# Attention and two FFN layers on one core: 128 operations get new ranks in a hand-run planner, with new planner durations, one early weight conversion instead of three, and a dummy activation

## The chip, the cores and the metric

The kernel runs on one core of a Trainium2 chip. The metric is the device time of one execution in microseconds (us), given as the median of the runs. One further execution was taken with the hardware profiler on; all rows below come from it.

## The reference

```python
scores = scale * q @ k.T                       # 4 batches, 8 heads, 576 x 576, head size 64
thresh = max(scores, -1) - tau                 # keep only scores near the row's maximum
attn = softmax(where(scores >= thresh, scores, -1e9))
x = (attn @ v) -> (2304, 512)                  # tokens x model
h = x @ w_in                                   # 512 x 2048
x = (h * sigmoid(1.702 * h)) @ w_out           # layer 1
h = x @ w_in2
out = (h * tanh(softplus(h))) @ w_out2         # layer 2
```

## The kernel before

Everything is float32; the FFN products are made from two fp32r parts each (a rounded part and the rest).

**Attention** runs over 72 groups: for each of 16 (batch, head pair) entries four full tiles of 128 queries of both heads, and for every second entry one mixed tile. A group has a score product on PE (L591), then for each of two heads on DVE a scaled copy with row minimum (L614), on POOL a threshold (L618), on ACT the exponential (L621), on DVE the masking with row sum (L624). Two groups later PE transposes the result (L660, L665), ACT copies it out of PSUM (L680), and PE multiplies it with v (L703, L728). Only one set of score banks exists, so the next group's L591 waits for both L614 of this one.

**The FFN layers** run over 48 pairs of 128-wide slices of the hidden layer, 24 for each layer, in 3 token blocks of 768 with 8 pairs each. A pair has seven products on PE (L829), copies and sums (L851, L843), the activation (L846), a split into two parts (L878, L881, L884), and the output product (L904 and L907, or L949).

**Weights** come as 64-bit words and are converted once by `conv_w` (L358): two ACT steps (L377, L379), two short DVE steps (L383, L386), one POOL step (L389), one DVE step (L391). `stage` (L408) converts the two halves of a pair and stores them to DRAM. `weights` (L418) either converts a pair of layer 1 in the ring `sv` (4 buffers, 2 to a pair) or loads it from DRAM (L427), and then splits it into the tiles `win` and `wout` (L444, L445, L449, L466, L467). `EARLY` says how many pairs are converted ahead: pair 0 through `weights`, pairs 1 and 2 through `stage` in the ring `sg`, each then loaded back into `sv`. `load_xs` (L499) loads, normalises and splits the tokens of a block.

**The order** of the work is made by the class `Order`. Each step is given to `add` with its engine, a duration, what it reads and writes, and a rank. `run` (L95) lets the steps run on a clock of its own: an engine that is free takes, of the steps that are ready, the one with the lowest rank; PE pays `TURN` for a change between score, transpose and product work; steps marked `port` on DVE and POOL exclude each other. `LAT` holds the delay from a step to a reader on another engine. The order that results is the order of issue on each engine; on the chip the engines wait for each other by semaphores, so the plan's times themselves don't reach the chip, only its order. Attention ranks are 0 to about 74, `load_xs(0)` has 80, FFN ranks start at 10000.

The lines on which the steps hang are L165, L421 and, for the dummy activation, the reads of "qsc" in L627:

```python
ready[a] = max(ready[a], end + lat + SLACK)
...
if n == 0 or len(EARLY) <= n < KP:
    vals = stage(1, k, rank, deps, svs)
...
    [kns, kn, kn + (1,), "qsc"], [kp, ksum + (col,)], rank, port=True)
```

Of the kernel before, what the change touches and what calls it, by code (L numbers as in the profile page):

```python
# [14 lines left out]
AF = mybir.ActivationFunctionType  # L15
# [17 lines left out]
FI = 20  # L33
HALF = 384
NHS = 4
SLACK = 0.0
AHEAD = 2
NSS = 6
EARLY = (1, 2, 3)
XR = 80  # L40
S0 = 8
S1 = 2
SR = 0.0
WR = 0.0


class Order:
# [7 lines left out]

    LAT = {
        "PE": {"PE": 0.0, "ACT": 0.27, "DVE": 0.2, "POOL": 0.27, "SP": 0.2},
        "DVE": {"PE": 0.26, "ACT": 0.13, "DVE": 0.13, "POOL": 0.16, "SP": 0.2},
        "ACT": {"PE": 0.22, "ACT": 0.08, "DVE": 0.15, "POOL": 0.16, "SP": 0.2},
        "POOL": {"PE": 0.22, "ACT": 0.08, "DVE": 0.15, "POOL": 0.1, "SP": 0.2},  # L60
        "SP": {"PE": 0.95, "ACT": 0.95, "DVE": 0.95, "POOL": 0.95, "SP": 0.95},
# [2 lines left out]
    def __init__(self):  # L64
        self.ops = []
        self.writer = {}
        self.readers = {}
        self.fill = None
        self.port = set()
        self.mode = {}  # L70

    def add(self, eng, dur, fn, r=(), w=(), rank=0.0, deps=(), nbytes=None, port=False, steps=1, mode=0):
        n = len(self.ops)
        if mode:
            self.mode[n] = mode
        if port:
            self.port.add(n)
        before = set(deps)
        for key in r:
            if key in self.writer:  # L80
                before.add(self.writer[key])
        for key in w:
            if key in self.writer:
                before.add(self.writer[key])
            before.update(self.readers.get(key, ()))
        for key in r:
            self.readers.setdefault(key, []).append(n)
        for key in w:
            self.writer[key] = n
            self.readers[key] = []  # L90
        before.discard(n)
        self.ops.append((eng, dur, fn, before, rank, nbytes, steps))
        return n

    def run(self):  # L95
# [20 lines left out]
        while done < n_ops:  # L116
# [45 lines left out]
            order.append((t, i))  # L162
            for a in after[i]:
                lat = self.LAT[e][self.ops[a][0]] if dur or nbytes else 0.0
                ready[a] = max(ready[a], end + lat + SLACK)  # L165
                left[a] -= 1
                if not left[a]:
                    heapq.heappush(future[self.ops[a][0]], (ready[a], a))
# [42 lines left out]
def attention_then_two_ffn_kernel(  # L211
# [86 lines left out]
    def t_mm(n, k=1):  # L298
        return k * (max(n, 256) * 0.4167e-3 + 0.0125)
# [4 lines left out]
    def t_act(n, ptr=0, psum=True):  # L304
        return (0.05 if psum else 0.09) + n * 0.833e-3 + 0.093 * ptr
# [262 lines left out]
    def qk(tl, rank):  # L568
# [6 lines left out]
        def mm():  # L575
# [18 lines left out]
                yield  # L594

        add("PE", 1.02, mm, [h[2] for h in kqt], [("sc", i) for i in range(4)], rank,
            steps=4 if full else 10, mode=1)
        return [(sc[i][:, :, 0:SH], [("sc", 2 * i), ("sc", 2 * i + 1)]) for i in range(2)]

    def softmax_a(sums, ksum, col, rank, bank, pair, i):  # L600
# [196 lines left out]
        reopen("g", i, [("p", i)] + ([("pmt", i)] if i < 2 else []))  # L797
    for i in range(3):
        reopen("x2", i, [("vr", i)])
    open_hb = add("SP", 0.0, open_h, deps=scored, rank=-10.0)  # L800
    load_xs(0, XR)
    for n, at in enumerate(EARLY):
# [12 lines left out]
    def hidden(n, rank):  # L815
# [16 lines left out]
                    yield  # L832

        def product(p, dst, kd, start):
            i = add("PE", t_mm(HALF, 6) + 0.03, lambda: mm(p, dst, start),
                    [("xq", p), ("win", n % 3, p)], [kd], rank + PO[p] / 8, [open_hb] if n == 0 else [], steps=6)
            firsts.setdefault(n, i)

        def h(i, j, x, kx, y=None, ky=None):
            ht, kh = hs[i]  # L840
            cs = slice(j * HALF, (j + 1) * HALF)
            if y is not None:
                add("DVE", t_dve(HALF), lambda: nc.vector.tensor_tensor(ht[:, cs], x(), y, ALU.add),  # L843
                    [kx, ky], [kh + (j,)], rank - 4.0)
            add("ACT", t_act(HALF),
                lambda: nc.scalar.activation(ht[:, cs], x() if y is None else ht[:, cs], fn),  # L846
                [kx] if y is None else [], [kh + (j,)], rank - 4.0)

# [86 lines left out]
    def out2(n, rank):  # L935
# [6 lines left out]
        for q, (i, ts) in enumerate(order):  # L942
            g, kg = units[i]

            def mm(i=i, ts=ts, g=g):
# [7 lines left out]
                        )  # L953
                        yield

            add("PE", 3 * len(ts) * t_mm(512), mm, kg + [("wout", n % 3)], [ka2[t] for t in ts],
                rank + (q + 0.5) / len(order), steps=3 * len(ts))
        if k == KP - 1:
            for t in range(6):
# [82 lines left out]
```

## Time and profile before

| | us |
|---|---|
| median of 3 runs | 1038.72 |
| lowest and highest | 1037.98, 1039.24 |
| profiled execution, its own time | 1037.93 |
| its span, first to last instruction | 1036.2 |
| PE busy | 1020.9 (99%) |
| DVE busy | 832.7 (80%) |
| ACT busy | 659.7 (64%) |
| POOL busy | 168.7 (16%) |

The time of the profiled execution is 1.7 us over its span. The granted clock is full throughout. PE's matmuls are pipelined, and the ends of their records are modelled, so a busy PE may still lose time between two matmuls; the waits of its weight loads (PEld) show such places. Times in rows are us from the span's start.

### The profile page before, as it was taken

How to read it: one execution, taken by the hardware profiler on the slowest of the kernel's cores; microseconds unless marked ns; L12 is line 12 of the kernel's file. 1: busy time of each engine (PE TensorE's matmuls, PEld its weight loads, DVE VectorE, ACT ScalarE, POOL GpSimd, SP SyncE). 2: the span in 40 equal slices, each digit the busy share in tenths (PEclk: the TensorE clock that was granted, in tenths of full speed). 3: DMA queues.
4: the chain of work that ended last, by engine and by line, in shares of the span. 5: the costliest groups of instructions: out<-in, count | busy, mean ns of one | idle time of the engine just before them, and what ended most of it. 6: DMA issues, size and time to landing. Idle time of an engine off the chain costs nothing.

```text
span 1036.2 us, 17403 instructions
## 1 busy us (share of the span) xinstructions
PE 1020.9 (99%) x6348; PEld 866.9 (84%) x6348; DVE 832.7 (80%) x1642; ACT 659.7 (64%) x1261; POOL 168.7 (16%) x182
## 2 busy tenths in 40 slices
PE   9999999999999999999999999999999999999998
PEld 6666666666698999999999999988889889889887
DVE  7999999999877889888798888865688665975633
ACT  5988787887866668666687667744464444544421
POOL 2543543333122210111211112000000000000000
PEclk9999999999999999999999999999999999999999
DMA  5434556443145536756376534612125112142001
GB/s 196 126 143 160 175 188 196 131 131 94 45 131 182 180 122 236 250 170 222 134 264 219 203 107 164 199 64 79 63 90 173 62 61 82 46 138 82 21 1 61
DMA packets 55942, 139.62 MB, mean 135 GB/s; under 512 B 8496, under 2 KB 18736, under 8 KB 55856
## 3 DMA queue, kind: packets, MB, share of 16 engines
q1 hardware_dynamic: 55856, 138.51, 39.8%
q8 instruction: 49, 0.80, 0.3%
q14 instruction: 37, 0.30, 0.1%
HBM read 107.48 MB, written 31.01 MB: 134 GB/s over the span
## 4 chain that ended last, share of the span: by engine, by line
PE 80%; ACT 8%; DVE 7%; DMA 2%; issue 1%; POOL 1%; SPq 0%; DVEq 0%; ACTq 0%; POOLq 0%
PE h L829 27%; PE tb L949 13%; PE tb L904 8%; PE sc L591 7%; PE tb L703 7%; PE h L949 6%; PE tb L665 6%; PE h L907 4%; DMA sv<-w_d 1%; PE tb L728 1%; DVE hs L843 1%; DVE xq L520 1%; ACT wout1a L680 1%; ACT sr L379 1%; ACT hs L846 1%
## 5 line engine op out<-in xcount | busy, mean ns | idle before, releaser
L843 DVE TENSOR_TENSOR hs<-h,u 128x384 f32<-128x384 f32 x144 | 79.7, 553 | 78.1 <-ACT u L851 54.5
L829 PE MATMUL h<-xq,win 128*128 128x384 f32 x672 | 131.5, 336 | 2.4 <-ACT u L851 2.2
L829 PE MATMUL h<-xq,win2b 128*128 128x384 f32 x672 | 131.7, 335 | 1.9 <-DVE hs L843 1.5
L829 PE MATMUL h<-xq,win1b 128*128 128x384 f32 x672 | 131.4, 335 | 0.0
L846 ACT ACTIVATE hs<-hs 128x384 f32<-128x384 f32 x144 | 75.9, 527 | 78.9 <-DVE hs L843 77.6
L829 PEld LDWEIGHTS h<-xq,win2b 128*128 128x128 f32 x672 | 116.0, 188 | 8.4 <-DVE hs L843 1.8
L829 PEld LDWEIGHTS h<-xq,win 128*128 128x128 f32 x672 | 115.6, 188 | 8.4 <-ACT u L851 2.9
L829 PEld LDWEIGHTS h<-xq,win1b 128*128 128x128 f32 x672 | 115.9, 188 | 5.6
L851 ACT COPY u<-h 128x384 f32<-128x384 f32 x144 | 68.6, 476 | 78.5 <-PE h L829 78.1
L614 DVE TENSOR_SCALAR_CACHE_REDUCE win2a<-sc,nqsc 128x576 f32<-128x576 f32 x144 | 111.4, 810 | 4.4 <-PE sc L591 4.0
L618 POOL TENSOR_SCALAR nm<-nm,tau_p 128x1 f32<-128x1 f32 x144 | 86.1, 599 | 159.6 <-DVE win2a L614 158.3
L591 PE MATMUL sc<-win1a 64*128 64x288 f32 (+3 forms) x672 | 91.8, 414 | 0.8 <-DVE win2a L614 0.7
L389 POOL TENSOR_TENSOR sg<-sg,sr 128x1024 uint32<-128x1024 uint32 x20 | 51.9, 2594 | 226.7 <-DVE sg L386 225.2
L449 DVE TENSOR_TENSOR sv<-sv 128x256 f32<-128x256 f32 x192 | 84.1, 442 | 0.2
L591 PEld LDWEIGHTS sc<-win1a 64*128 64x128 f32 (+1 forms) x672 | 52.2, 173 | 28.3 <-DVE win2a L614 9.4
L444 ACT CAST win2b<-sv 128x256 fp32r<-128x256 f32 (+1 forms) x96 | 41.9, 442 | 33.6 <-DVE sv L449 28.1
L444 ACT CAST win<-sv 128x256 fp32r<-128x256 f32 (+1 forms) x96 | 42.2, 448 | 30.2 <-DVE sv L449 26.6
L444 ACT CAST win1b<-sv 128x256 fp32r<-128x256 f32 (+1 forms) x96 | 42.1, 444 | 29.4 <-DVE sv L449 23.6
L445 DVE TENSOR_TENSOR win<-sv,win 128x256 fp32r<-128x256 f32 (+1 forms) x96 | 48.9, 512 | 9.7 <-ACT win L444 9.5
L445 DVE TENSOR_TENSOR win2b<-sv,win2b 128x256 fp32r<-128x256 f32 (+1 forms) x96 | 45.9, 479 | 13.5 <-ACT win2b L444 13.4
L445 DVE TENSOR_TENSOR win1b<-sv,win1b 128x256 fp32r<-128x256 f32 (+1 forms) x96 | 44.1, 462 | 11.9 <-ACT win1b L444 11.7
L680 ACT COPY wout1a<-tb 128x512 f32<-128x512 f32 x72 | 40.7, 598 | 11.6 <-PE tb L665 11.3
(242 smaller groups left out, 2283.7 us busy)
## 6 DMA issues: line engine op xcount, KB each, us to landing
sv<-w_d SPq DMA_DIRECT2D x84, 512.0 KB
sr<-in_w_in SPq DMA_DIRECT2D x16, 1024.0 KB
sr<-in_w_out SPq DMA_DIRECT2D x32, 512.0 KB
w_d<-sg SPq DMA_DIRECT2D x20, 512.0 KB
win1a<-in_kq SPq DMA_DIRECT2D x16, 576.0 KB
xr<-x_d SPq DMA_DIRECT2D x24, 384.0 KB
w_d<-sv SPq DMA_DIRECT2D x12, 512.0 KB
x_d<-xo SPq DMA_DIRECT2D x16, 288.0 KB
```

The lines of the kernel that those rows point to most:

```text
L444: add("ACT", t_act(256 * m, psum=False), lambda: nc.scalar.copy(at(0), src), [ku] + pre_in, keys, rank)
L445: add("DVE", t_dve(256 * m), lambda: nc.vector.tensor_tensor(at(1), src, at(0), ALU.subtract), [ku], keys, rank, port=True)
L449: add("DVE", t_dve(256), lambda: nc.vector.tensor_tensor(out, x, y, op), [], [ku], rank, port=True)
L591: nc.tensor.matmul(sc[i][at:at + m, g, c0:c0 + n], kq2[rows, q0:q0 + m], kq2[rows, k0:k0 + n], start=True, stop=True)
L614: lambda: nc.vector.tensor_scalar(n3, s3, nqsc, None, ALU.mult, ALU.min, accum_out=nm[:, 0:1]),
L618: lambda: nc.gpsimd.tensor_scalar(nm[:, 1:2], nm[:, 0:1], tau_p, 0.0, ALU.add, ALU.add),
L703: nc.tensor.matmul(av[64 * i:64 * i + 64], vr[:, vc:vc + 64], p[:, a:a + 256], start=(c == 0), stop=(c == 4))
L829: nc.tensor.matmul(dst(), w[:, h, c], xq[p][:, x, cs], start=(start and i == 0), stop=(p in (5, 6) and i == 5), skip_group_check=True)
L843: add("DVE", t_dve(HALF), lambda: nc.vector.tensor_tensor(ht[:, cs], x(), y, ALU.add), [kx, ky], [kh + (j,)], rank - 4.0)
L846: lambda: nc.scalar.activation(ht[:, cs], x() if y is None else ht[:, cs], fn),
L904: nc.tensor.matmul(acc2[e](), w[:, x], g(y)[:, 0:512], start=first, stop=last, skip_group_check=True)
L949: nc.tensor.matmul(acc2[t](), g(x)[:, t * 128:(t + 1) * 128], w[:, y], start=(k == i == j == 0), stop=(k == KP - 1 and i == 1 and j == 2), ...
```

## The change

Five things, all of them in what the planner is told, but for the dummy activation.

1. `NUDGE` adds an amount (a number of eighths) to the rank of 128 steps, named by their place in the list of steps. 96 of them have places below 1385 and so are steps of attention, most of them transposes and products on PE; the amounts reach from -5.75 to +8 ranks there. The others are spread over the loads, conversions and FFN pairs.
2. Durations: the delay from DVE to DVE goes from 0.13 to 0, from DVE to POOL from 0.16 to 0.2; a score product's readers may be planned 0.1 earlier (`soon`); L829 and L949 get 0.024 less and 0.006 more; the first activation of layer 2 is planned 1.28 longer.
3. `EARLY` is (1,): pairs 1 and 2 are converted by `weights` in `sv`, without a load back from DRAM. Their stores to DRAM remain, since blocks 2 and 3 read them.
4. A dummy activation with the function of layer 1 on the small tile `nqsc`. It is planned with rank 1000 and writes "qsc", so it comes behind the last L624 and ahead of all steps of rank 10000.
5. `SLACK`, which was 0, is gone.

```diff
-SLACK = 0.0
-EARLY = (1, 2, 3)
+EARLY = (1,)
+GR = 1e3
+NUDGE = {
+    6: 26, 20: -1, 33: 18, 34: -28, 66: 13, 68: 5, 73: 12, 75: -1, 79: -3, 84: -2, 88: 2, 101: 18,
...
+    1328: 30, 1338: -5, 1347: 64, 1353: 12, 1363: 15, 1399: 9, 1444: 14, 1492: 1, 1502: 4, 1541: -3,
...
+    -32, 4243: -3, 4255: 14, 4260: -1,
+}
-        "DVE": {"PE": 0.26, "ACT": 0.13, "DVE": 0.13, "POOL": 0.16, "SP": 0.2},
+        "DVE": {"PE": 0.26, "ACT": 0.13, "DVE": 0.0, "POOL": 0.2, "SP": 0.2},
+        if soon:
+            self.soon[n] = soon
+        rank += NUDGE.get(n, 0) / 8
-                ready[a] = max(ready[a], end + lat + SLACK)
+                ready[a] = max(ready[a], end + lat - self.soon.get(i, 0.0))
         add("PE", 1.02, mm, [h[2] for h in kqt], [("sc", i) for i in range(4)], rank,
-            steps=4 if full else 10, mode=1)
+            steps=4 if full else 10, mode=1, soon=0.1)
+    add("ACT", 1.5, lambda: nc.scalar.activation(nqsc, nqsc, AF.Gelu_apprx_sigmoid), w=["qsc"], rank=GR)
-            i = add("PE", t_mm(HALF, 6) + 0.03, lambda: mm(p, dst, start),
+            i = add("PE", t_mm(HALF, 6) + 0.006, lambda: mm(p, dst, start),
-            add("ACT", t_act(HALF),
+            add("ACT", t_act(HALF) + (1.28 if n == NPAIR and (i, j) == (0, 0) else 0.0),
-            add("PE", 3 * len(ts) * t_mm(512), mm, kg + [("wout", n % 3)], [ka2[t] for t in ts],
+            add("PE", 3 * len(ts) * (t_mm(512) + 0.0057), mm, kg + [("wout", n % 3)], [ka2[t] for t in ts],
```

## Rows read from the trace of the kernel before

**Rows 1.** Busy time by stretch: us, PE, PEld, DVE, ACT, POOL, clock, DMA.

```profile
0.00:30.00 30.00, 27.76 (x183) 19.33 (x185) 22.68 (x81) 19.62 (x34) 7.73 (x19) 1.00 0.46 169
30.00:270.00 240.00, 235.76 (x2063) 155.46 (x2060) 237.00 (x599) 197.58 (x396) 94.28 (x138) 1.00 0.46 147
270.00:345.00 75.00, 70.82 (x447) 64.74 (x446) 58.93 (x93) 53.11 (x95) 16.19 (x7) 1.00 0.43 139
345.00:1031.00 686.00, 685.26 (x3657) 626.65 (x3656) 512.66 (x870) 389.38 (x740) 50.53 (x20) 1.00 0.38 128
```

**Rows 2.** Waits from 30 to 270: who, for whom, us, times, longest.

```profile
PEld tb L665 <- issue: 12.5, 33, 0.4
PEld sc L591 <- DVE win2a L614: 7.2, 21, 0.5
```

**Rows 3.** DVE groups from 30 to 270: busy, mean ns, idle before.

```profile
L614 DVE TENSOR_SCALAR_CACHE_REDUCE win2a<-sc,nqsc 128x576 f32<-128x576 f32 x130 | 100.6, 809 | 1.2 <-PE sc L591 0.8
L624 DVE SCALAR_TENSOR_TENSOR g2a<-win2a,nm,g2a 128x577 f32<-128x577 f32 x34 | 28.1, 840 | 0.7 <-ACT g2a L621 0.5
L624 DVE SCALAR_TENSOR_TENSOR g3a<-win2a,nm,g3a 128x577 f32<-128x577 f32 x33 | 28.1, 860 | 0.4 <-ACT g3a L621 0.4
L624 DVE SCALAR_TENSOR_TENSOR g1a<-win2a,nm,g1a 128x577 f32<-128x577 f32 x32 | 26.7, 838 | 0.5 <-ACT g1a L621 0.5
L624 DVE SCALAR_TENSOR_TENSOR g0a<-win2a,nm,g0a 128x577 f32<-128x577 f32 x32 | 26.3, 828 | 0.3 <-ACT g0a L621 0.3
L391 DVE SCALAR_TENSOR_TENSOR sg<-sr,sg 128x1024 uint32<-128x1024 uint32 x4 | 4.9, 1216 | 0.0
L383 DVE TENSOR_SCALAR sg<-sg 128x1024 f32<-128x1024 f32 x4 | 2.7, 680 | 0.0
L386 DVE TENSOR_SCALAR sg<-sg 128x1024 uint32<-128x1024 uint32 x4 | 2.7, 675 | 0.0
```

**Rows 4.** PE in order of time at the two longest waits: start, us, idle before.

```profile
283.32 2.35 PE L829 MATMUL h<-xq,win 128*128 128x384 f32 x12 [2.16 <-ACT u L851]
...
315.28 1.31 PE L829 MATMUL h<-xq,win2b 128*128 128x384 f32 x6 [1.52 <-DVE hs L843]
```

**Rows 5.** ACT in order of time around the first wait.

```profile
276.37 1.18 ACT L377 ACTIVATE sv<-sr 128x1024 f32<-128x1024 f32 x1
...
278.16 0.21 ACT L735 COPY xo<-tb 128x64 f32<-128x64 f32 x1 [0.25 <-PE tb L728]
278.39 1.28 ACT L846 ACT_TABLE_LOAD   x1
279.69 0.53 ACT L846 ACTIVATE hs<-hs 128x384 f32<-128x384 f32 x1
...
281.77 1.14 ACT L379 ACTIVATE sr<-sr 128x1024 f32<-128x1024 uint32 x1
282.80 0.47 ACT L851 COPY u<-h 128x384 f32<-128x384 f32 x1
```

**Rows 6.** DVE and POOL around the second wait.

```profile
311.29 3.46 DVE L391 SCALAR_TENSOR_TENSOR sv<-sr,sv 128x1024 uint32<-128x1024 uint32 x1
...
311.17 2.49 POOL L389 TENSOR_TENSOR sv<-sv,sr 128x1024 uint32<-128x1024 uint32 x1 [1.96 <-ACT win L444]
```

**Rows 7.** DVE: last early conversion, last mask, end of pair 3's conversion.

```profile
147.94 1.22 DVE L391 SCALAR_TENSOR_TENSOR sg<-sr,sg 128x1024 uint32<-128x1024 uint32 x1
...
270.05 0.81 DVE L624 SCALAR_TENSOR_TENSOR g3a<-win2a,nm,g3a 128x577 f32<-128x577 f32 x1
...
295.21 1.22 DVE L391 SCALAR_TENSOR_TENSOR sv<-sr,sv 128x1024 uint32<-128x1024 uint32 x1 [2.58 <-POOL sv L389]
```

**Rows 8.** PE, first products of pairs 1 and 2, and SP, first load back.

```profile
285.51 2.24 PE L829 MATMUL h<-xq,win1b 128*128 128x384 f32 x12
...
301.11 1.20 PE L829 MATMUL h<-xq,win2b 128*128 128x384 f32 x6
...
97.25 0.32 SPq L427 DMA_DIRECT2D sv<-w_d  x1
```

## What the change should do to the time

> **What bounds the kernel now.** I read the busy times by stretch first, then the waits, then the groups of DVE, then the chain of steps at the few places where PE stands.
>
> The stretches [rows 1] show three kinds of work. From 345 to 1031 the FFN pairs run with PE busy 685.26 of 686.00 us: 0.74 us are idle, and no order of steps can give back more than that there, as long as each matmul takes what it takes now. From 30 to 270 is attention. PE idles 240.00 - 235.76 = 4.24 us and DVE 240.00 - 237.00 = 3.00 us: two engines are full at once, each waiting for the other for moments. From 270 to 345 the one goes over into the other, and PE idles 75.00 - 70.82 = 4.18 us; two waits are most of it, 2.16 us at 283.32 and 1.52 us at 315.28 [rows 4]. The first 30 us have 2.24 us of idle PE, part of it before the first data. So the idle time that an order of steps can win is some 8 us, in attention and the crossing.
>
> A busy PE in attention hides more, for its weight loads wait inside it: 33 waits of a transpose's load with no releaser add up to 12.5 us, about 0.38 each, where the kind of work changes, and 21 waits of score products for L614 to 7.2 us [rows 2]. Beside that, PEld is busy 155.46 of 240 us in attention against 626.65 of 686 in the FFN [rows 1]. The Trainium skill (Perfetto Trace Analysis, Identifying the Most-Contended Engine) calls matmul busy time a poor measure and wants the share of the weight loads instead: 65% against 91% here. By it attention would hold 155.46 / 0.91 = 171 us of PE work, and up to 69 us would be open, an estimate. The DVE row beside it speaks against such a gain: an order that gives PE more would meet a DVE that has 3.00 us left. So the sum goes by DVE.
>
> **The change part by part.** The sum is made against the profiled execution's own 1037.93 us (span 1036.2 and 1.7 around it); the median of the runs, 1038.72, lies 0.79 over it, and I add that at the end.
>
> *One early conversion.* Nothing is converted less or more often: pairs 1 and 2 had their conversion in `sg` and get it in `sv`. A half costs DVE 0.68 + 0.68 + 1.22 = 2.58 us (L383, L386, L391) [rows 3], a pair 5.2, both pairs 10.3, and POOL four L389 of about 2.5 [rows 6]. What goes is four loads back from DRAM, 0.32 us of SP's issue each [rows 8]; SP has no wait that PE shows. The stores stay, each behind its L391 on SP as before. The conversions are work for gaps before (lowest priority, done at 147.94 + 1.22 = 149.2 [rows 7]) and after (rank 10001 and 10002 in place of 5001 and 5002, both behind all of attention). Buffers allow it too: pair 1 takes the two of `sv` that are free, pair 2 the two that pair 0's split leaves. I take 0, between a gain of 1.3 us (the four issues) and the loss that stands as a rival below.
>
> *Dummy activation.* The table load for the layer's function takes 1.28 us on ACT and now lies at 278.39, right ahead of the first activation [rows 5]. ACT runs without a gap from there to the copy L851 at 282.80, which ends the 2.16 us wait of PE [rows 4, 5]. Taken out of that stretch, 1.28 us of the 2.16 fall away, if nothing else holds that copy. The load comes back behind the last L624, which starts at 270.05 [rows 7], and with an activation of its own. Behind it on ACT stand the last tiles' L680 copies, which PE's products wait for; ACT's work grows by some 0.2. There PE has FFN products of pair 0 to fill in with. I take -1.3, between -2.16 (the whole wait goes) and +1.3 (the copies are late by the load, and PE too).
>
> The Trainium skill (ScalarE: Activation LUTs, What ACT_TABLE_LOAD costs) gives 2.66 us for a switch, 1.38 of it a drain behind the load. Here the copy before ends at 278.37, the load runs from 278.39 to 279.67, and the activation starts at 279.69 [rows 5]: no drain stands in that place. By the page the term would be -2.16, the whole wait, 0.9 more than I take.
>
> *Planner's durations.* They do no work on the chip; they change which step the plan takes first. The second long wait shows what a wrong clock costs: L391 took 3.46 us instead of 1.22, since POOL's L389 ran beside it from 311.17 to 313.66, and L843 behind it held PE for 1.52 us [rows 4, 6]. The plan excludes such pairs (`port`), so on the chip the two had drifted together. With a new order this meeting is as likely to be gone as not, and others can come up; I take half, -0.7, between -1.5 and +1.5 for a new one.
>
> *The moved ranks.* 96 of 128 are in attention. The ceiling is DVE's: 3.00 us idle [rows 1], and what L624 is drawn out over the 0.809 us of L614, which is as wide and has no partner on POOL: 34 x 0.031 + 33 x 0.051 + 32 x 0.029 + 32 x 0.019 = 4.3 us [rows 3]. Together 7.3. From PE's side the idle time is 4.24 [rows 1]. I take -4.0, next to PE's row, since a wait that stops PE is what an order can be built around; the bounds are -7.3 and +2, the latter half of PE's idle time again for an order that fits the chip worse. In the FFN 0.74 us is all there is, so 0. The last pair's products are moved by up to 4 ranks, but PE is not idle there.
>
> Sum: 0 - 1.3 - 0.7 - 4.0 = -6.0. Profiled execution 1031.9, median 1038.72 - 6.0 = 1032.7. What is late next is DVE in attention, which then stands near full.
>
> **The rivals.**
>
> *Fillers leave attention.* Weight conversions could drop out of the full stretch of DVE into 270 to 345, where it idles 75.00 - 58.93 = 16.07 us [rows 1]. Of the 10.3 us for pairs 1 and 2 half would then shorten attention, as PE's changes of work (0.38 us each) can shrink with it: another -5.2, 1027.5. For it: `weights` puts no mark on them. Against it: only three of the moved ranks belong to those conversions, by at most 13 eighths, and a free DVE takes them in attention's gaps as before.
>
> *The order wins only on the planner's clock.* The chip's waits of 0.2 to 0.5 us are not in it one by one, and 128 steps fitted to a plan may win there and nowhere else. Then only the table load and chance remain: 1038.72 - 1.3 = 1037.4. For it: L391's 3.46 us, which the plan didn't have.
>
> *Slower: pair 2's conversion comes after attention.* In `sv` it needs pair 0's buffers, and its rank is higher than before. Pair 3's conversion has that place now: from 276.37 [rows 5] to 295.21 + 1.22 = 296.4 [rows 7], 20.1 us for two halves. If pair 2 took that place, pair 3 would follow 20.1 later, at 316.5, with some 5.3 us of splitting behind (my estimate, as much DVE time as its conversion): 321.8. PE begins pairs 285.51 and 301.11 apart by 15.6 [rows 8] and wants pair 3 at 316.7. It would wait 5.1 us; with the table load's -1.3, 1042.5. This decides as soon as pair 2's last L391 lies behind about 276. For it: nothing forces the conversion early any more. Against it: the gaps that took it until 149.2 are still there, with 120 us to spare until 270.
>
> That the change does not do what it says can show in one point: if the compiled code loads the table again ahead of L846, -1.3 turns to +1.3, 1035.3; it stays in the forecast's range.
>
> **How the numbers follow.** The forecast with its bounds around (1029 to 1036.6) gets 0.56, fillers leaving 0.19, the order that wins on the planner's clock alone 0.14, slower 0.11. The measurement can tell about 0.2%, 2.1 us: faster is below 1036.6. The first two are faster, 0.75; the third lies within, 0.14; the fourth above 1040.8, 0.11. The range runs from 1027, just under the second case, to 1038.7, over the third; it leaves out the slow one and the tail of the large gain.
>
> **What would show it.** Right: from 30 to about 266 both DVE and PE idle less than 4 us; attention's last L624 some 4 us before 270.05; a table load ahead of the first L846 by several us, and no wait of PE near 2 us at the first pair; FFN pairs 15.6 us apart as before, and 0.7 us of idle PE there. Wrong: the last L624 at 270 as before (then the ranks won nothing); conversions of pair 2 behind 276 and PE waiting for `win` at pair 2 or 3 (the slow rival); conversions of pairs 1 and 2 outside attention and no such wait (the large gain); a new L391 or L445 of over 2 us beside L389 with PE waiting behind it.

## The result, and the profile after

The changed kernel takes 1047.22 us (median of 4 runs, 1046.68 to 1048.65) against 1038.42 (1037.98 to 1039.24) for the kernel before, run in turn with it: ratio 1.0086 [1.0068, 1.0103], slower by 8.8 us where 6.0 less was forecast. Its profiled execution took 1047.55 us with a span of 1045.8.

Busy time by stretch, kernel after (us, PE, PEld, DVE, ACT, POOL, clock, DMA share, GB/s), beside [rows 1]:

```profile
0.00:30.00 30.00, 26.89 (x187) 19.31 (x187) 22.69 (x81) 19.20 (x34) 7.45 (x21) 1.00 0.46 169
30.00:270.00 240.00, 234.66 (x2039) 153.62 (x2035) 231.23 (x590) 196.61 (x392) 94.36 (x136) 1.00 0.39 125
270.00:345.00 75.00, 73.06 (x469) 65.27 (x467) 66.77 (x104) 55.34 (x99) 16.02 (x7) 1.00 0.52 167
345.00:1031.00 686.00, 680.12 (x3620) 620.95 (x3619) 522.06 (x865) 389.97 (x741) 54.25 (x20) 1.00 0.38 129
```

In the window of the crossing (270 to 345) PE's idle time falls from 4.18 to 1.94. Attention won nothing: DVE now idles 8.77 us, not 3.00, and PE 5.34, not 4.24. The FFN, where 0.74 us were idle, now idles 5.88. Set side by side, the first products of pairs 0, 3, 12, 13 and 24 start 1.2 us earlier and 0.4, 5.2, 8.3 and 9.5 later than before, and the last matmul ends 9.8 later. So nearly all of the loss shows between pairs 3 and 24, the stretch in which the weights of later pairs are converted beside the products; whether attention should have gained more is a question of its own.

The same view of 290 to 660 for the kernel before, then after:

```profile
290.00:660.00 370.00, 367.55 (x2113) 342.63 (x2112) 313.43 (x489) 261.57 (x467) 64.28 (x25) 1.00 0.54 187
```
```profile
290.00:660.00 370.00, 362.90 (x2066) 336.70 (x2065) 320.01 (x476) 257.58 (x454) 70.19 (x26) 1.00 0.54 185
```

Fewer matmuls are done (2066, not 2113), while DVE is busier with fewer steps (320.01 us for 476, not 313.43 for 489): its steps got longer. PE's waits there, after (who, for whom: us, times, longest):

```profile
PE h L850 <- ACT u L872: 5.1, 5, 2.0
PE h L850 <- DVE hs L864: 1.8, 3, 0.8
```

Lines stand 20 or 21 further down than before: L850 is the product L829, L872 the copy L851, L864 the add L843; of the splitting, L464 and L465 are L444 and L445, L469 is L449, L487 is L467; L905 is the split L884, L928 the output product L907; L409 is POOL's add L389 ("the add" from here on), L411 the step L391 behind it. In attention L611, L634 and L644 are L591, L614 and L624, and L723 and L732 the product L703 and its copy L712. In some experiments a line stands one to three further down again. Two of these waits are about 2 us long. The one that costs more, in order of time, after, by engine (start, us, idle before): DVE, POOL, ACT, PE.

```profile
454.80 1.22 DVE L487 TENSOR_TENSOR wout<-sv,wout 128x1024 fp32r<-128x1024 f32 x1
455.93 3.25 DVE L465 TENSOR_TENSOR win1b<-sv,win1b 128x512 fp32r<-128x512 f32 x2
459.22 0.42 DVE L469 TENSOR_TENSOR sv<-sv 128x256 f32<-128x256 f32 x1
...
455.02 3.29 POOL L409 TENSOR_TENSOR sg<-sg,sr 128x1024 uint32<-128x1024 uint32 x1 [4.75 <-DVE sg L406]
...
459.68 0.41 ACT L464 CAST win1b<-sv 128x256 fp32r<-128x256 f32 x1 [4.55 <-DVE sv L469]
460.96 0.41 ACT L464 CAST win1b<-sv 128x256 fp32r<-128x256 f32 x1 [0.87 <-DVE sv L469]
461.27 0.47 ACT L872 COPY u<-h 128x384 f32<-128x384 f32 x1
...
459.66 0.28 PE L928 MATMUL h<-g1b,wout1b 128*128 128x256 f32 x1
461.79 1.07 PE L850 MATMUL h<-xq,win2b 128*128 128x384 f32 x3 [1.85 <-ACT u L872]
```

POOL's add begins as soon as its input is there, and ends at 455.02 + 3.29 = 458.31. DVE's two L465, 1.03 us otherwise, take 3.25: the first begins inside the add and ends only at 458.86, behind it. L469 behind them on DVE is late, two L464 on ACT wait for it, and the copy that frees PE's bank (a part of PSUM, the memory into which PE writes its products) stands behind them in ACT's fixed order. None of these steps is urgent but the last. PE's clock falls too:

```profile
459.00:462.00 3.00, 1.15 (x7) 0.79 (x6) 2.96 (x7) 1.19 (x3) 0.00 (x0) 1.00 0.02 8
462.00:464.00 2.00, 2.00 (x7) 1.95 (x7) 2.00 (x5) 1.07 (x3) 0.00 (x0) 0.53 0.10 31
464.00:466.00 2.00, 2.00 (x9) 1.76 (x8) 1.25 (x2) 1.18 (x2) 0.00 (x0) 0.61 0.22 53
```

After 1.85 us without work the granted clock is 0.53 and 0.61 of the full 2.4 GHz for 4 us (mostly the 1.2 GHz level), which costs 2 x 0.47 + 2 x 0.39 = 1.7 us. Wait and clock together are some 3.6. Not every execution has this: the profiled one has a mean clock of 0.998, but the two of the four at 1.000 took 1046.68 and 1046.88 us, still 8.3 and more above the kernel before.

### The profile page after: what moved, and what is told of

The parts are those of the page before. It is cut to its first block, busy times and chain, and to the rows that moved or that the text cites. A ratio compares the mean times of both kernels' runs of the same rounds, so it can differ in the third digit from the quotient of the medians.

```text
span 1045.8 us, 17360 instructions
## 1 busy us (share of the span) xinstructions
PE 1025.8 (98%) x6354; PEld 868.0 (83%) x6354; DVE 847.3 (81%) x1642; ACT 661.1 (63%) x1262; POOL 172.1 (16%) x182
## 4 chain that ended last, share of the span: by engine, by line
PE 80%; DVE 8%; ACT 6%; DMA 4%; issue 1%; SPq 0%; POOL 0%; DVEq 0%; ACTq 0%; POOLq 0%
PE h L850 26%; PE tb L970 12%; PE sc L611 8%; PE tb L723 8%; PE tb L925 8%; PE tb L685 6%; PE h L970 6%; PE h L928 4%; DMA sv<-w_d 1%; PE tb L680 1%; DVE sv L469 1%; PE tb L748 1%; DVE win1b L465 1%; DMA sr<-in_w_in 1%; ACT hs L867 1%
## 5 line engine op out<-in xcount | busy, mean ns | idle before, releaser
L864 DVE TENSOR_TENSOR hs<-h,u 128x384 f32<-128x384 f32 x144 | 79.7, 554 | 81.1 <-ACT u L872 57.8
L850 PE MATMUL h<-xq,win2b 128*128 128x384 f32 x672 | 132.7, 337 | 4.9 <-ACT u L872 4.5
L850 PE MATMUL h<-xq,win 128*128 128x384 f32 x672 | 132.6, 336 | 1.3 <-ACT u L872 0.7
L850 PE MATMUL h<-xq,win1b 128*128 128x384 f32 x672 | 132.0, 336 | 0.9 <-DVE hs L864 0.8
L850 PEld LDWEIGHTS h<-xq,win2b 128*128 128x128 f32 x672 | 116.4, 189 | 11.6 <-ACT u L872 5.4
L850 PEld LDWEIGHTS h<-xq,win 128*128 128x128 f32 x672 | 115.5, 188 | 7.9 <-DVE hs L864 1.5
L850 PEld LDWEIGHTS h<-xq,win1b 128*128 128x128 f32 x672 | 115.7, 188 | 7.3 <-DVE hs L864 1.4
L634 DVE TENSOR_SCALAR_CACHE_REDUCE win2a<-sc,nqsc 128x576 f32<-128x576 f32 x144 | 111.8, 812 | 10.5 <-PE sc L611 10.3
L872 ACT COPY u<-h 128x384 f32<-128x384 f32 x144 | 68.7, 477 | 79.0 <-PE h L850 78.6
L611 PE MATMUL sc<-win1a 64*128 64x288 f32 (+3 forms) x672 | 90.1, 413 | 0.2 <-DMA win1a<-in_kq 0.2
L469 DVE TENSOR_TENSOR sv<-sv 128x256 f32<-128x256 f32 x192 | 88.9, 464 | 1.2
L409 POOL TENSOR_TENSOR sg<-sg,sr 128x1024 uint32<-128x1024 uint32 x16 | 44.0, 2749 | 224.3 <-DVE sg L406 144.5
L611 PEld LDWEIGHTS sc<-win1a 64*128 64x128 f32 (+1 forms) x672 | 51.1, 173 | 25.4 <-issue 10.2
L464 ACT CAST win<-sv 128x256 fp32r<-128x256 f32 (+1 forms) x96 | 42.3, 444 | 41.5 <-DVE sv L469 34.2
L464 ACT CAST win1b<-sv 128x256 fp32r<-128x256 f32 (+1 forms) x96 | 42.1, 442 | 35.7 <-DVE sv L469 28.2
L464 ACT CAST win2b<-sv 128x256 fp32r<-128x256 f32 (+1 forms) x96 | 42.1, 441 | 28.3 <-DVE sv L469 21.8
L409 POOL TENSOR_TENSOR sv<-sv,sr 128x1024 uint32<-128x1024 uint32 x16 | 42.6, 2667 | 84.0 <-ACT u L872 29.5
L465 DVE TENSOR_TENSOR win1b<-sv,win1b 128x256 fp32r<-128x256 f32 (+1 forms) x96 | 51.6, 541 | 5.0 <-ACT win1b L464 4.9
L465 DVE TENSOR_TENSOR win2b<-sv,win2b 128x256 fp32r<-128x256 f32 (+1 forms) x96 | 46.7, 488 | 10.2 <-ACT win2b L464 9.9
L465 DVE TENSOR_TENSOR win<-sv,win 128x256 fp32r<-128x256 f32 (+1 forms) x96 | 48.4, 506 | 7.6 <-ACT win L464 7.5
```

The costliest lines, as they stand in the source:

```text
L409: lambda: nc.gpsimd.tensor_tensor(bits, bits, word(0), ALU.add), keys, [kval], rank, port=True)
L464: add("ACT", t_act(256 * m, psum=False), lambda: nc.scalar.copy(at(0), src), [ku] + pre_in, keys, rank)
L465: add("DVE", t_dve(256 * m), lambda: nc.vector.tensor_tensor(at(1), src, at(0), ALU.subtract), [ku], keys, rank, port=True)
L469: add("DVE", t_dve(256), lambda: nc.vector.tensor_tensor(out, x, y, op), [], [ku], rank, port=True)
L611: nc.tensor.matmul(sc[i][at:at + m, g, c0:c0 + n], kq2[rows, q0:q0 + m], kq2[rows, k0:k0 + n], start=True, stop=True)
L634: lambda: nc.vector.tensor_scalar(n3, s3, nqsc, None, ALU.mult, ALU.min, accum_out=nm[:, 0:1]),
```

## The experiments

Two theories stood at the start. **Port:** DVE's steps with two operands in SBUF (and L383, with one) are drawn out while POOL's add runs. Counting every DVE step that takes over 0.1 us more than the median of its line and shape, the excess adds up to 34.4 us in the kernel before and 41.4 after, and all of it falls beside an add (the expectations below count some 3 us less, 30.8 and 38.6). Steps that read PSUM are not touched: in the kernel before L614 and L843 began inside an add 20 times, and none was drawn out. `port` in the plan keeps the two apart, but makes nothing wait on the chip. **Bank:** at six places in attention a product stands right behind another on PE and waits for ACT's copy out of the same bank (after: PE, ACT, PE):

```profile
201.29 0.59 PE L723 MATMUL tb<-wout2a,x22a 128*64 128x256 f32 x2
...
201.92 0.37 ACT L732 COPY xo<-tb 128x256 f32<-128x256 f32 x1 [1.11 <-PE tb L723]
...
202.35 1.08 PE L723 MATMUL tb<-wout2a,x22a 128*64 128x256 f32 x6 [0.46 <-ACT xo L732]
```

**The add made narrow**, in the changed kernel and in the one before:

```diff
-            lambda: nc.gpsimd.tensor_tensor(bits, bits, word(0), ALU.add), keys, [kval], rank, port=True)
+            lambda: nc.gpsimd.tensor_tensor(bits[:, 0:8], bits[:, 0:8], word(0)[:, 0:8], ALU.add), keys, [kval], rank, port=True)
...
-                bits, word(1), 0x80000000, bits, ALU.bitwise_and, ALU.bitwise_or),
+                bits, word(1), 0x80000000, bits, ALU.bitwise_and, ALU.bitwise_and),
```

The second edit, in L411, leaves zeros, so all weights are zero: this part of the computation is left out.

> The changed kernel, its plan and all its orders kept, but POOL's add in the weight conversion (L409) works on 8 of 1024 columns, and the step behind it (L411) leaves zeros, so all weights are zero and the output isn't the reference's. Theory A (in the FFN of layer 1 DVE is held while L409 runs, at places where PE then waits): the changed kernel lost 8.6 us between its pairs 1 and 24 against the kernel before, where it idles 5.1 + 1.8 us for ACT and DVE from 290 to 660; without a long L409 these waits go, and the time falls from 1047.2 by 7 to 11 us, to 1036 to 1040, with FFN pairs 15.6 us apart throughout. Theory B (the loss was made in attention, by PE's order): the time falls by at most 3 us, to 1044 or more.

> The kernel before with the same edit (L389 narrow, all weights zero), its plan and orders kept. Theory A: its waits of PE for a held DVE are few (1.5 us at 315, 0.2 at 331, 0.3 at 400, small ones behind), so it falls by 2 to 5 us only, to 1033 to 1036.5, and the distance between the two kernels shrinks from 8.8 to 2 to 5 us. Theory B: it falls by as much as the changed kernel, and the distance stays 8 to 9 us.

Measured: 1035.93, ratio 0.9977 [0.9968, 0.9987], and 1033.89, 0.9958 [0.9943, 0.9973]; 11.3 less than the changed kernel and 4.3 less than the 1038.19 of before in the same runs. Their distance of 8.8 shrinks to 2.0. The order is the same with either add, so the same product can be looked up in both traces: the changed kernel is level with its narrow twin (the same kernel with the narrow add) to 300 us, then falls behind by 0.9 at 300, 5.3 at 413, 6.5 at 445, 10.2 at 466 and 12.0 at 660; 3.7 of it at the place shown above. The kernel before loses 5.2 in the same way, 3.6 of it behind 300. The zero weights don't make the products faster: where nothing waits, a pair of layer 1 takes 15.6 us in both.

The stretch with the conversions, changed kernel, narrow add; then one group of DVE in it (busy, mean ns), with the whole add and with the narrow one:

```profile
290.00:660.00 370.00, 370.00 (x2136) 346.66 (x2135) 294.59 (x498) 267.22 (x475) 10.86 (x26) 1.00 0.56 192
```
```profile
L905 DVE TENSOR_TENSOR g1b<-hs,g1b 128x768 fp32r<-128x768 f32 x12 | 17.6, 1465 | 0.5 <-ACT g1b L899 0.5
```
```profile
L905 DVE TENSOR_TENSOR g1b<-hs,g1b 128x768 fp32r<-128x768 f32 x12 | 11.5, 957 | 1.2 <-ACT g1b L899 1.2
```

PE has no idle time at all, and the same place reads (DVE, ACT):

```profile
448.98 1.03 DVE L465 TENSOR_TENSOR win1b<-sv,win1b 128x512 fp32r<-128x512 f32 x2
...
452.39 0.48 ACT L872 COPY u<-h 128x384 f32<-128x384 f32 x1 [0.20 <-PE h L850]
```

The copy waits for PE now, not for the splitting. The run takes away the add's own length together with what it does to DVE, so it shows that POOL's add carries the loss, not yet how.

**The bank.** At the six places the copy reads another tile (the right values are left out there); then that with the narrow add.

```diff
-        add("ACT", t_act(256), lambda: nc.scalar.copy(x[:, at:at + 256], av), [kav],
+        src = vr[:, 0:256] if len(sch.ops) in (333, 643, 955, 989, 1162, 1335) else av
+        add("ACT", t_act(256), lambda: nc.scalar.copy(x[:, at:at + 256], src), [kav],
```

> The changed kernel with its plan and orders kept; six of the 32 copies L732 (those of the products that another product follows directly on PE) read an SBUF tile instead of PSUM bank tb3, so 256 columns of six tiles of attention are wrong. Theory C (PE's second matmul of the next product waits for the copy out of the same bank, although the two use different halves of it): the six gaps of 0.84 us at 84.6, 144.4, 201.5, 209.7, 245.8 and 274.9 shrink to 0.2, and 6 x 0.64 = 3.8 us go, less what DVE holds back: 1043 to 1045.5. Rival (the waits are covered, DVE sets the pace of attention): within 1 us of 1047.2, last L644 no earlier.

> Both edits in the changed kernel (narrow L409 with zero weights, six copies from SBUF). If A and C are two independent causes, their gains add: 1047.2 less 9 and less 3, about 1035, at or below the kernel before with narrow L389. If they are one (a delay from attention only shifts the meetings of POOL and DVE), the gain is no larger than that of the narrow L409 alone.

Measured: 1046.39, 1.0078 [1.0061, 1.0095], and 1033.10, 0.9947 [0.9932, 0.9962]: -0.8 and -2.8. Taken so, the bank seemed to be hidden. But set product against product the six copies gain 0.7 to 1.1 us at each place and lose 4.1 behind one, at 88 us (ACT, PE, then the clock there):

```profile
87.89 0.40 ACT L733 COPY xo<-x20a 128x256 f32<-128x256 f32 x1 [2.81 <-DMA x20a<-in_v]
...
89.84 0.33 PE L680 MATMUL tb<-ident,g0a 128*128 128x128 f32 x1 [2.34 <-ACT g0a L700]
```
```profile
90.00:92.00 2.00, 2.00 (x15) 1.33 (x16) 2.00 (x7) 1.67 (x5) 0.29 (x1) 0.80 0.00 0
92.00:96.00 4.00, 4.00 (x23) 2.24 (x21) 2.98 (x10) 1.79 (x5) 0.84 (x2) 0.67 0.02 4
```

The tile that the copy reads in its place had not landed: the experiment made a stall of its own. So the first place, 333, was left out:

> The changed kernel with the copy reading another tile at five of the six places where a product waits for it (all but the first; what the copies read is wrong at these places, so the output is too). In the kernel of the six copies the stand-in tile had not yet landed at the first place: there ACT waited 2.81 us for its DMA, PE 2.34 us behind that, and PE's clock stood at 0.80 and 0.67 for the 6 us behind, some 3.6 us in all, a loss of the experiment and not of the change. If the bank waits cost what the matched products of the two kernels show place by place (0.6 to 1.1 each behind the first), this kernel takes 1042 to 1044. If they are mostly hidden, as the 0.8 of the six copies seemed to say, it stays at 1046 to 1047.5.

Measured: 1042.28, 1.0038 [1.0025, 1.0051], -4.9 against the changed kernel; of that, product against product, 4.2 are won by the end of attention, 0.5 are lost again at 300, and 1.5 are won at 465, where PE waits as long (1.85 us) but keeps its clock. So some 3.7 are the banks', and the rest hangs on the clock.

```profile
30.00:270.00 240.00, 236.53 (x2068) 156.20 (x2070) 235.23 (x598) 200.52 (x399) 94.98 (x137) 1.00 0.40 128
```

PE idles 3.47 us in attention, not 5.34, and the last score product starts at 262.9: 3.5 earlier than in the changed kernel, and 2.1 earlier than in the kernel before (1.2 earlier than in the changed kernel without ranks, below, where it starts at 264.1).

**The parts one by one.** The changed kernel without the ranks, and with the ranks of operations below 1385 only (attention; these are 90 of the 128, not 96, and 38 are left); the kernel before with one early conversion, with the dummy activation, with all the new durations, with its two DVE latencies alone.

```diff
-        rank += NUDGE.get(n, 0) / 8
+        rank += 0.0
```

> The changed kernel without the 128 moved ranks (NUDGE adds 0); durations, one early conversion and dummy activation stay. If the moved ranks made the loss (they put steps of DVE right where L409 runs on the chip, and products next to each other in one bank), this is near the kernel before: 1035 to 1040, DVE lengthened beside L409 from 290 to 660 by about 24 us as before instead of 35, and no gap of 0.84 between products. If the new durations or the early conversion made it, it stays at 1044 to 1049.

```diff
-        rank += NUDGE.get(n, 0) / 8
+        rank += NUDGE.get(n, 0) / 8 if n < 1385 else 0.0
```

> The changed kernel with only the moved ranks of attention (places below 1385); those of loads, conversions and FFN pairs add 0. If the loss of 8 us in layer 1 comes from the ranks given to steps of layer 1 themselves, it goes and some 1038 to 1041 is left (attention's own loss of 3 us stays, with its gaps between products). If attention's ranks do it by where they leave the conversions, it stays at 1045 or more.

```diff
-EARLY = (1, 2, 3)
+EARLY = (1,)
```

> The kernel before with EARLY = (1,) alone. My prediction put this at 0: 1036 to 1040.5, with the conversions of pairs 1 and 2 done in attention. The rival of the prediction (pair 2's conversion behind attention, PE waits for win): 1041 or more, with the last L391 of pair 2 behind 276.

```diff
+    add("ACT", 1.5, lambda: nc.scalar.activation(nqsc, nqsc, AF.Gelu_apprx_sigmoid), w=["qsc"], rank=1e3)
```

> The kernel before with the dummy activation alone. My prediction: 1.3 us faster, 1036.9, no table load between 276 and 284 ahead of L846 and a wait of PE at the first pair of about 0.9 instead of 2.16 us. Rival: the load stands in the way of the last copies L680 and PE waits there; 1038.2 or more.

```diff
-        "DVE": {"PE": 0.26, "ACT": 0.13, "DVE": 0.13, "POOL": 0.16, "SP": 0.2},
+        "DVE": {"PE": 0.26, "ACT": 0.13, "DVE": 0.0, "POOL": 0.2, "SP": 0.2},
...
-                ready[a] = max(ready[a], end + lat + SLACK)
+                ready[a] = max(ready[a], end + lat - self.soon.get(i, 0.0))
```

The first line alone is the kernel of the latencies; that of the durations has all of point 2 of the change.

> The kernel before with all the changed durations of the planner and nothing else (DVE to DVE 0.13 to 0.0, DVE to POOL 0.16 to 0.2, score products counted done 0.1 earlier, a product 0.024 shorter, an output product 0.0057 longer for each matmul, 1.28 on the first activation). Rival one, the prediction's own term: the durations move the time by -0.7, at most 1.5 either way, so 1037 to 1040. Rival two, what is left over by difference: the changed kernel without its moved ranks took 1040.87, the dummy activation alone gave -3.9 and the early conversions alone +1.2 against 1038.48, so if the parts add up, the durations cost 2.4 + 3.9 - 1.2 = 5.1 and this kernel takes about 1043.5. In that case DVE's steps that are drawn out beside POOL's add should sum to more than the kernel before has.

> The kernel before with two of the durations alone: DVE to DVE 0.13 to 0.0 and DVE to POOL 0.16 to 0.2. If the durations cost 5, these two are the ones that pack DVE's steps more closely in the plan and should carry most of it: about 1042. If it is the products' durations that matter, this stays at 1038.5 within 1.5 and the kernel with all durations doesn't.

| kernel | us | ratio to before | PE idle, 30 to 270 | PE idle, 290 to 660 |
|---|---|---|---|---|
| before | 1038.3 to 1038.5 | 1 | 4.24 | 2.45 |
| + early conversion | 1039.72 | 1.0013 [1.0003, 1.0022] | 6.16 | 0.84 |
| + dummy activation | 1034.55 | 0.9963 [0.9950, 0.9976] | 4.22 | 0.86 |
| + durations | 1041.97 | 1.0036 [1.0025, 1.0047] | 4.36 | 1.72 |
| + two latencies only | 1053.99 | 1.0152 [1.0135, 1.0168] | 9.55 | 7.22 |
| changed, no ranks | 1040.87 | 1.0026 [1.0016, 1.0036] | 4.72 | 4.84 |
| changed, attention's ranks | 1043.56 | 1.0050 [1.0035, 1.0065] | 4.00 | 3.88 |
| changed | 1047.22 | 1.0086 [1.0068, 1.0103] | 5.34 | 7.10 |

Alone the parts give +1.2, -3.9 and +3.7, +1.0 in sum; together, without ranks, 1040.87 - 1038.48 = +2.4. The ranks add 6.4: attention's 2.7, the 38 others 3.7. This split is a rough one: an order moved early shifts all that follows, and the four runs with attention's ranks lie from 1041.65 to 1044.56, the two at a mean clock of 1.000 at 1041.65 and 1043.02. They bring the bank waits: none without ranks, two with attention's, six with all of them. They don't bring the meetings of DVE and POOL: from 290 to 660 DVE's steps are drawn out by 28.0 us before, by 35.8 in the changed kernel without ranks, where as little as before was expected, and by 37.8 with them. Yet PE's idle time there goes from 4.84 to 7.10 with the ranks, so they change what stands behind such a step. Two latencies, a part of the durations, cost more alone (15.7, which neither expectation had) than all durations: the terms don't add up, each is another draw of the order. The kernel with the dummy activation beats both kernels; its load (ACT) and PE's first waits:

```profile
271.31 1.28 ACT L800 ACT_TABLE_LOAD   x1
272.60 0.20 ACT L800 ACTIVATE nqsc<-nqsc 128x1 f32<-128x1 f32 x1
...
275.27 0.56 ACT L847 ACTIVATE hs<-hs 128x384 f32<-128x384 f32 x1
```
```profile
281.28 2.38 PE L830 MATMUL h<-xq,win 128*128 128x384 f32 x12 [0.68 <-ACT u L852]
286.78 0.50 PE L905 MATMUL tb<-g0b,wout 128*128 128x512 f32 x1 [0.66 <-DVE g0b L885]
```

These two are the longest from 270 to 345, where 2.16 and 1.52 stood [rows 4].

**Can the plan be told of the port?** On the chip the add starts as soon as its input is there; in the plan DVE, asked first, could put it off. So POOL is asked first:

```diff
-        engines = sorted({o[0] for o in self.ops})
+        engines = sorted({o[0] for o in self.ops}, key=lambda e: (e != "POOL", e))
```

> The kernel before with the dummy activation, and with one line of the planner changed: of engines that are free at the same moment it asks POOL first, so that in the plan POOL's add takes the shared port as soon as its input is there, as it does on the chip, and DVE's steps with two operands in SBUF are planned around it. If the plan's wrong picture of the port costs time, DVE's steps drawn out beside POOL's add sum to less than in the kernel before (30.8 us) and the time falls below the 1034.55 of the dummy activation alone, by up to the 2 us that the kernel before lost to the port and the dummy activation didn't already win back: 1032 to 1034. If POOL's add in the plan only blocks DVE where DVE could have gone first, the time stays or rises by 1 to 2: 1034.5 to 1036.5.

> The changed kernel with POOL asked first, and nothing else changed; its moved ranks were found for the other plan, so they fit this one by chance only. If the port's wrong picture is what loses the time, this comes down from 1047.2 towards the 1035.9 of the changed kernel with a narrow add, by half or more: 1036 to 1042. If the loss lies in the ranks and durations as such, it stays at 1043 to 1047.

Measured: 1046.02, 1.0066 [1.0051, 1.0081], and 1059.77, 1.0204 [1.0189, 1.0219]: 11.5 and 12.6 above the same kernels without it. Both lie above what was expected. DVE's steps are drawn out less (28.3 us where 30.5 stood with the dummy activation, 33.2 where 41.4 stood), yet PE waits more. So the sum of what DVE loses isn't what is paid; it matters what stands behind it. But the runs don't show that a plan can't be told of the port: by its own clock, too, the new plan is 8.7 and 21.7 us longer (table at the end of this section), so this edit made a worse plan as well as another picture of the port.

**The add in four pieces**, same order, all work done:

```diff
-            lambda: nc.gpsimd.tensor_tensor(bits, bits, word(0), ALU.add), keys, [kval], rank, port=True)
+            lambda: [nc.gpsimd.tensor_tensor(bits[:, c:c + n // 4], bits[:, c:c + n // 4], word(0)[:, c:c + n // 4], ALU.add)
+                     for c in range(0, n, n // 4)], keys, [kval], rank, port=True)
```

> The changed kernel with POOL's add issued as four adds of 256 columns in place of one of 1024; all work is done, and the planner's order is the same. If a DVE step is held until POOL's running instruction ends, it now gets through after a quarter of the add (0.6 us in place of up to 2.45): DVE's steps drawn out by over 0.1 us sum to 20 or less in place of 38.6, the FFN's waits shrink with them, and the time falls to 1037 to 1042. If DVE is held as long as POOL has adds queued, or if it is slowed to POOL's pace however the add is cut, the sum stays near 38 and the time at 1046 to 1049.

> The kernel before with the dummy activation and with the add in four pieces. By the first theory it falls below the 1034.55 of the dummy activation alone, towards 1031 to 1034; by the second it stays at 1034 to 1036.

Measured: 1045.54, 1.0070 [1.0055, 1.0085], and 1035.98, 0.9977 [0.9968, 0.9986]. DVE is held until POOL's running instruction ends, and no longer: its steps are drawn out by 17.4 us in place of 41.4. But the time hardly moves, for the gain comes back as a wait of DVE for the add, which has become longer (DVE's waits from 290 to 660, then DVE and POOL at the place shown above, changed kernel in four pieces):

```profile
DVE sv L412 <- POOL sv L409: 11.0, 7, 2.1
DVE sg L412 <- POOL sg L409: 9.3, 5, 2.3
```
```profile
454.54 2.13 DVE L466 TENSOR_TENSOR win1b<-sv,win1b 128x512 fp32r<-128x512 f32 x2
...
453.72 4.43 POOL L409 TENSOR_TENSOR sg<-sg,sr 128x256 uint32<-128x256 uint32 x4 [4.16 <-ACT u L873]
```

20.3 us of waiting (1.5 with the whole add) stand for the 24.0 of lengthening that went, and the 32 adds keep POOL busy for 118.9 us in place of 86.6. DVE pays for POOL's use of SBUF in the one form or the other. The Trainium skill (Advanced Engine Details and Errata, Miscellaneous Facts) says that POOL shares a read and a write interface with DVE, in conflict with DVE's steps of two SBUF inputs and with those in a two-port mode. The trace agrees for two inputs, with L469 drawn out from 0.42 to 2.63 us at 408.09; L383, which has one input, was drawn out from 0.69 to 1.61 us at 29.11 before, and whether that is the two-port mode no run here shows.

**Are the amounts better than chance?** The same 128 amounts dealt out at random among the same operations, twice, and the first deal with the narrow add.

> The changed kernel with the same 128 operations moved by the same 128 amounts, but dealt out among them at random. If the search found amounts that fit the chip in part, a random deal is slower than the 1047.2 of the changed kernel: 1049 to 1056. If the search's gain was made on the planner's clock alone, a random deal does as the searched one: 1043 to 1049. If moving ranks costs nothing by itself and the searched amounts are to blame, it is close to the 1040.9 of the changed kernel without them.

> A second random deal of the same 128 amounts among the same 128 operations. The first took 1053.75, 6.5 above the searched deal. If the searched amounts fit the chip in part, this one too lies above 1047.2, at 1049 to 1058; if the first deal was bad luck and search and chance do alike, it lies at 1041 to 1049.

> The same random deal with POOL's add on 8 of 1024 columns (weights become zero; this part of the computation is left out). With the searched amounts the narrow add took the changed kernel to 1035.9. If the port is how a new order loses time, this comes to 1036 to 1039, whatever the kernel with the whole add takes; if a random deal loses in attention, where the port hardly shows, most of its distance stays.

Measured: 1053.75, 1.0150 [1.0133, 1.0167]; 1052.00, 1.0136 [1.0119, 1.0153]; narrow 1043.69, 1.0052 [1.0037, 1.0067]. The kernel's own amounts are 4.8 and 6.5 better on the chip than two deals of chance; but all three stand above no moved ranks at all, 1040.87. The narrow add takes 10.1 from the first deal and leaves it 7.8 above the changed kernel with a narrow add, where 1036 to 1039 was expected of the port alone: that order also loses elsewhere. Against the narrow twin it is 2.4 late at attention's last score product (268.9, not 266.5), loses 3.9 between pair 3's first product and the last matmul, and 2.8 behind that.

**What the plan itself promised.** `run` comes to an end on its own clock (`self.last`). Worked out from the kernels' texts (us):

| kernel | the plan's end | on the chip |
|---|---|---|
| before | 1035.6 | 1038.4 |
| + dummy activation | 1036.9 | 1034.55 |
| + dummy activation, POOL first | 1045.6 | 1046.02 |
| changed, no ranks | 1032.4 | 1040.87 |
| changed, attention's ranks | 1029.1 | 1043.56 |
| changed | 1023.2 | 1047.22 |
| changed, the two deals | 1040.9, 1036.5 | 1053.75, 1052.00 |
| changed, POOL first | 1044.9 | 1059.77 |

By the plan the change wins 12.4 us, 9.2 of them by the ranks; on the chip the ranks lose 6.4. The chip lies 2.8 us above the plan before, 8.5 in the changed kernel without ranks, 12.9 and 15.5 with the deals and 24.0 with the kernel's own amounts (these plans use the new durations). Moved ranks widen the distance, and those that the plan likes best widen it most. The plan does know something, for it too puts the deals behind the kernel's own amounts; it leaves out that an add holds DVE, and that two products share a bank.

## Why the prediction was wrong, point by point

**What bounds the kernel** was read rightly, the FFN by PE, attention by PE and DVE at once, but the FFN's limit was used in one direction only. "0.74 us is all there is, so 0" is a ceiling on the gain; it says nothing of the loss. A stage with no idle time has nothing to win and all to lose when the order of its fillers changes. This is the step that failed most: the FFN's term was put at 0, and the FFN went from 0.74 to 5.88 us idle, in the profiled execution another 1.7 went with the clock, and POOL's add carried 11.3 us in all where it had carried 4.3.

**Moved ranks, -4.0, bounds -7.3 to +2:** all 128 together cost 6.4, outside the bounds; attention's alone 2.7, which the runs don't tell from +2. There was something to win: with five of the six bank waits gone the last score product comes 2.1 earlier than before, though 0.9 of it comes without any ranks. What failed is the step from PE's idle time to a gain that PE may keep: the ranks put products L723 right behind each other that share a bank, a wait that the plan does not know, since it keeps the two halves of the bank apart. The trace of before has it not once for these products, but it does have it, twice, for the short products of the mixed tiles, so it could have been priced:

```profile
82.98 0.45 PE L728 MATMUL tb<-wout2a,x20a 128*64 128x64 f32 x8 [0.31 <-ACT xo L735]
```

The ceiling on DVE's side was misread in part. The 4.3 us by which L624 is drawn out over L614 are POOL's add: five L624 that began inside an add lost 3.9 us in the kernel before, while L614 runs beside adds too and loses nothing. After, from 30 to 270 (the second row answers [rows 3], where L614 waits 0.8 for PE):

```profile
PEld tb L723 <- ACT xo L732: 4.8, 6, 0.9
DVE win2a L634 <- PE sc L611: 7.0, 12, 1.2
```

The last mask step, due some 4 us before 270.05, starts at 272.88.

**Planner's durations, -0.7, bounds 1.5 either way:** alone +3.7. The sign named for being wrong, a new L391 or L445 of over 2 us beside POOL's add with PE waiting behind it, is what came (the rows above). The step that failed is that one meeting of the two was priced: DVE lost 29.5 us to such meetings from 270 on before the change and 37.8 after it, over 18 and 20 steps, and a new order deals all of them anew. Of the +3.7 of the durations alone some 1.7 are the clock, which was 0.50 from 287 to 289 and 0.67 to 291.

**Dummy activation, -1.3, bounds -2.16 to +1.3:** right in mechanism, mis-sized; alone -3.9. It took 1.48 us from the first wait, and the second, 1.52, which the sum had put down to the durations, gave way to one of 0.66. The rest lies in the order behind it: pair 3 starts 2.8 us earlier, the last matmul ends 3.4 earlier. The load is not issued twice. The Trainium skill (ScalarE: Activation LUTs, What ACT_TABLE_LOAD costs) adds a drain of 1.38 us to a load. It doesn't show: 271.31 + 1.28 = 272.59, and the activation starts at 272.60.

**One early conversion, 0:** alone +1.2, where only four issues or a late conversion had a price. PE's clock accounts for it: in the profiled execution it stands at 0.50 from 287 to 289 and at 0.75 to 291, behind the wait of 2.2 us that the kernel before has too, there at 1.00. Nine of the ten runs have a mean clock of 0.998; the one at 1.000 took 1037.44, no more than before. So the term itself may have been right, and what was left out is that a wait of PE can cost clock behind it. In the changed kernel the slow rival did not happen: pair 2's last L411 starts at 269.94, before the 276 from which it decides. With this part alone PE idles 6.16 us in attention, against 4.24. Its waits of L703 for ACT's copies L680 grow from 1.4 us over 6 to 2.8 over 13; why these copies come later stays open.

**The account.** Taken away one at a time, the share of POOL's add grew by 11.3 - 4.3 = 7.0 and the bank waits cost 4.9, together 11.9; the measured 8.8 leaves -3.1 for the rest, beside the dummy activation's -3.9 alone. Since the parts don't add up exactly, and some of the clock's loss is in both terms, this is an account and no proof of each term. Shown is that the add and the banks carry the loss; why the new order puts more of PE's copies behind an add is not.

**The rivals.** Slower came, by none of those named: the slow rival's 5.1 us belong to a conversion that did not come late. "The order wins only on the planner's clock" was nearest: the plan promises 12.4 us and the chip gives none of it. But it let such an order cost nothing; its 1037.4 rests on that.

## What to carry to other kernels

Where an engine is full, its idle time bounds what a new order can win, but not what it can lose: look for the queues in which a step for that engine stands behind fillers (work without urgency), and for resources that the plan leaves out, and price those. When an order is fitted to a plan, compare the plan's promise with the chip's time: a growing distance can mean that the order was fitted to what the plan has wrong. An exclusion that stands only in a planner's model does not hold on the chip, and here cutting the intruder in pieces turned the hold into a wait. Put a sure edit, such as a table load moved into a slack stretch, in by itself: alone it gave 3.9 us here, and with a reshuffled order it was lost.

## What the hardware showed

A DVE step of two SBUF operands that begins inside POOL's add ends behind the add: L469, 0.42 us, took 2.63; L905, 0.95, took 2.59; two L465 3.25 for 1.03. It ends 0.3 to 1.1 us behind the add, about its own length, as if held and then run. Steps that read PSUM (L614, L843) ran beside the add at their usual length. Between two products that share a bank, 0.84 us pass from the start of the last matmul to the start of the next, while ACT copies the other half in 0.37 us. A wait of PE of 1.85 us at 460 was followed by 4 us at about half its clock (0.53 and 0.61); after one of 2.02 at 409, and after the same one of 1.85 in the kernel of the five copies, the clock stayed at 1.00 (the changed kernel, then that of the five copies):

```profile
412.00:415.00 3.00, 3.00 (x19) 2.88 (x18) 2.04 (x5) 3.00 (x7) 0.00 (x0) 1.00 0.28 109
```
```profile
459.00:462.00 3.00, 3.00 (x19) 2.83 (x18) 2.72 (x5) 2.37 (x5) 0.00 (x0) 1.00 0.16 49
```

So one late copy can cost nearly twice its wait, or just that.
